# One group of a local-attention kernel with its weights as the stationary operand, and layernorm passes on ScalarE

## The chip, the core and the metric

The kernel runs on one core of a Trainium2 chip. Its engines have names of their own in the profile: PE is TensorE (PEld is its weight load), DVE is VectorE, ACT is ScalarE, POOL is GpSimd, and SP issues most DMAs. The metric is the time of one execution on the device in microseconds, as the median of several runs. Lower is better.

## What is computed

The input x has 2048 rows of 640 numbers, in fp32. Each row is normalised, xn = (x - mean) / sqrt(var + eps). From xn come two branches:

```
qkv  = xn @ wqkv                      # 640 x 1920, 32 heads of 20
each row attends to 8 rows: itself and those 2, 4, ... 14 rows above
s    = attention(q, k, v) @ wo        # 640 x 640
g    = silu( silu(xn @ w1) @ w2 )     # 640 x 1536, 1536 x 640
out  = x + s * g
```

## The kernel before

The 2048 rows are dealt out to four groups of 512 rows, and a group is 4 tiles of 128 rows (T = 4, tile index t). A tile takes every 8th row, so that the 8 rows that a row attends to lie in the same partition of neighbouring tiles or a partition or two above.

For each group the order on TensorE is: the q, k, v product in four quarters (`qkv_phase`), then the output projection of the group before (`wo_phase`), then the FFN (`ffn_phase`). The last group's projection stands at the end by itself (`wo_last`). The attention itself is VectorE's work (products, reductions, sums), spread over the time in which TensorE does the next products.

Precision is kept by splitting. Each operand is a high half of a type that TensorE multiplies fast and a low half that holds what is left. A product is three matmuls: high x high, low x high, high x low. The halves of the activations are TH, TL (normalised input), OH, OL (attention output) and sh, sl (hidden activations); those of the weights stand side by side in a ring of seven buffers `w`. In their first use the weights' halves are made by ScalarE (L463, the high half) and VectorE or POOL (L466, the low half) and stored to DRAM; later uses load the stored halves (L451, on POOL's queue).

In the FFN the first product (`up`, L972 to L974) has the weights stationary and 512 rows of the group moving, 15 matmuls of 512 columns for each of the 12 chunks of 128 hidden units. ScalarE makes silu of the result twice, as the high half sh and in full as sf (L978, L979), and VectorE subtracts to get sl (L980). The second product (`down`) comes for two chunks at a time and has the activations stationary: for each tile t, 640 columns of w2 move in two matmuls, 384 wide (L853) and 256 wide (L856), with the same stationary tile loaded for each. Its result is in rows, over six PSUM banks. The projection has the same form. The result of `down` goes through silu into the tile G (L1027); in `wo_phase` VectorE multiplies the projection into G (L895), POOL adds x (L901), and SP stores the rows (L903).

The next group's x is loaded in the FFN's second pair of chunks. VectorE takes statistics (L500, L502), ScalarE the square root (L506), VectorE applies mean and factor (`ln_apply`, L512). `turn_x` turns the result: VectorE transposes blocks of 32 x 32 (L555), ScalarE moves blocks between partitions (`move`, L540) and makes TH (L524), VectorE makes TL (L525). Attention output is turned the same way in `turn_o` (L567, L540, L524, L525).

The order on each engine is not written out. `Weave` collects the operations with a duration, the tiles read and written and a priority, plays them through in a model, and hands them to the engines in the order in which they started there. TensorE keeps the program's order. Each engine then runs its list strictly in order. A low priority number goes first among operations that could start; layernorm has LN_AT = 55, attention 100 and more, moves 3000.

Of the kernel before, what the change touches and what calls it, by code (L numbers as in the profile page):

```python
# [40 lines left out]
NB = P // B  # L41
SHIFT = 16
RUN = D
X_AT = 1.5, 3.5, 5.5
LOW_AT = 3
ON_DVE = (3, 6, 7, 8)
# [17 lines left out]
def tsl(t):  # L64
    return slice(t * P, (t + 1) * P)
# [175 lines left out]
def local_attention_silu_ffn(ctx: ExitStack, tc: tile.TileContext, x, wqkv, wo, w1, w2, out):  # L241
# [196 lines left out]
    def w_load():  # L438
        i = loaded[0]
        if i >= len(units):  # L440
            return
        loaded[0] += 1
        u, s = units[i], i % RING
        n = width(u)
        r = WR[s]
        both = r[:, :2 * n]
        kh, kl = ("wh", s), ("wl", s)
        due = clock[0]
        if what[i] == "load":
            src = halves[u]  # L450
            add("POOL", 1.0, lambda: nc.gpsimd.dma_start(both, src), [("half", u)], [kh, kl], due + 10,  # L451
                nbytes=2 * n * P * 4)
            return
        k = fresh.index(i)
        if not k:
            raw_load(0)
            rawn[0] = 1
        raw, kr = raws.pop(i)
        early_raw.append((raw, kr))
        hi, lo = r[:, :n], r[:, n:2 * n]  # L460
        if len(raw.shape) > 2:
            hi, lo = (v.rearrange("p (c f) -> p c f", c=DC) for v in (hi, lo))
        act(n, lambda: nc.scalar.activation(hi, raw, AF.Copy), kr, [kh], 1000 + due, name=f"wh{k}")  # L463
        pool_does = k < LO and k not in ON_DVE
        eng, cost, by = ("POOL", po(n), nc.gpsimd) if pool_does else ("DVE", dv(n), nc.vector)
        add(eng, cost, lambda: by.tensor_tensor(  # L466
            out=lo, in0=raw, in1=hi.bitcast(F32), op=OP.subtract), [kh] + kr, [kl],
            due if pool_does else LOW_AT if k < LO else 50, lock=True, name=f"wl{k}")
        if what[i] == "store":
            kept = dram.tile([P, 2 * n], F32, name="half_" + "_".join(map(str, u)))  # L470
            halves[u] = kept
            dma(lambda: nc.sync.dma_start(kept, both.bitcast(F32)), [kh, kl], [("half", u)], 2 * n * P * 4,
                due + STORE)
        while rawn[0] <= (min(k + SLOTS - (k + 1) % 2, early - 1) if k < early - 2 else k + 4):
            raw_load(rawn[0])
            rawn[0] += 1
# [27 lines left out]
    def ln_rstd(a, b, at=1, after=(), name=None):  # L504
        n = range(a, b)
        act(b - a, lambda: nc.scalar.activation(SD[:, 0, a:b], MV[:, a:b, 1], AF.Sqrt, bias=epst, scale=1.0),  # L506
            [("mv", t) for t in n] + list(after), [("sd", t) for t in n], 0, "sqrt", name=name and "q" + name)
        dve(10, lambda: nc.vector.reciprocal(out=SD[:, 1, a:b], in_=SD[:, 0, a:b]),
            [("sd", t) for t in n], [("rs", t) for t in n], at, name=name and "r" + name)

    def ln_apply(t):
        dve(320, lambda: nc.vector.tensor_scalar(  # L512
# [362 lines left out]

    TM = mm(CA) + mm(CB)

    def wo_phase(g, i):
        banks = tm_banks(True)
        a, b = banks  # L880
        for c in range(DC):
# [15 lines left out]
        for t in range(T):  # L897
            s = take("xr", 2)
            xr = XR[s]
            dma(lambda t=t, xr=xr: nc.sync.dma_start(xr, rows(xg, g)[:, t, :]), [], [("xr", s)], P * D * 4, clock[0] + 5)  # L900
            add("POOL", po(D), lambda t=t, xr=xr: nc.gpsimd.tensor_tensor(out=xr, in0=xr, in1=G[:, t, :], op=OP.add),  # L901
                [("g", t, 0), ("g", t, CA)], [("xr", s)], 500, lock=True)
            dma(lambda t=t, xr=xr: nc.sync.dma_start(rows(og, g)[:, t, :], xr), [("xr", s)], [], P * D * 4, clock[0] + 20)  # L903

    def wo_last(g, i):
# [10 lines left out]

        def give(p, kp, t, cs):
            n = cs.stop - cs.start
            dve(n, lambda: nc.vector.tensor_tensor(out=G[:, t, cs], in0=p, in1=G[:, t, cs], op=OP.mult),
                [kp], [("g", t, cs.start)], 0)  # L920
            dve(n, lambda: nc.vector.tensor_tensor(out=xr[t][:, cs], in0=xr[t][:, cs], in1=G[:, t, cs], op=OP.add),
                [("g", t, cs.start)], [kx[t]], 0, lock=True)

        def leave(t, cs):
            dma(lambda: nc.sync.dma_start(rows(og, g)[:, t, cs], xr[t][:, cs]), [kx[t]], [], P * 4 * (cs.stop - cs.start), 0)

        def steps(cs):
            return [(OH, c, k) for c in cs for k in (0, 1)] + [(OL, c, 0) for c in cs]
# [29 lines left out]

    def ffn_phase(g, i, ix, io):
        nxt = g + 1 if g + 1 < NG else None  # L960
        ps = tm_banks()
        a, b = ps

        def up(f):
            wh, wl, kh, kl = w_next("w1", f)
# [3 lines left out]
            def first():  # L969
# [9 lines left out]
            act(TOK, lambda: nc.scalar.activation(sf, h, AF.Silu), [kp], [("sf", s)], 0, "silu")  # L979
            dve(TOK, lambda: nc.vector.tensor_tensor(out=sl, in0=sf, in1=sh.bitcast(F32), op=OP.subtract),  # L980
                [("sf", s), ("sh", s)], [("sl", s)], 0, lock=True)

        def down(fs):
            ws = {f: w_next("w2", f) for f in fs}
# [26 lines left out]
        for f in range(0, FC, 2):  # L1011
# [5 lines left out]
            if nxt is not None and f == X_IN:  # L1017
                for t in range(T):
                    ln_stats(t)
                ln_rstd(0, T, after=[("sf", 1)])  # L1020
                for t in range(T):
                    ln_apply(t)
                turn_x(g, ix)
            down((f, f + 1))
        for p, kp, ts, cs in tm_views(ps, "aaaabb" if nxt is not None else "abaaab"):
            n = (ts.stop - ts.start) * (cs.stop - cs.start)
            act(n, lambda p=p, ts=ts, cs=cs: nc.scalar.activation(G[:, ts, cs], p, AF.Silu), [kp], gkeys(ts, cs), 0.1 if nxt is None else -1, "silu")  # L1027
# [4 lines left out]
    for g in range(NG):  # L1032
        other = 1 - slot
        qkv_phase(g, slot, other)
        if g:
            wo_phase(g - 1, other)
        ffn_phase(g, slot, other, other)
        if g < NG - 1:
            slot = other
# [30 lines left out]
```

## Time and profile before

| | |
|---|---|
| median of 3 runs | 618.46 us (618.18 to 618.94) |
| profiled execution | 618.66 us, span 616.9 us from first to last instruction |
| busy: PE, PEld, DVE, ACT, POOL | 611.0, 551.1, 563.5, 310.4, 110.3 us |
| granted TensorE clock, mean | 0.999 |
| group 0: its FFN, the projection of its rows | 61.06 to 143.39 us, 194.65 to 211.85 us |
| last group: FFN's end and last projection | to 595.9 us, then to 613.3 us |

How to read it: a matmul's duration in the profile runs into the next one's, so a block's length is read from one start to a later start. The chain of waits is the way back from the last instruction through whatever released each step. A row of grouped instructions gives line, engine, operation, tiles, shape and count, then busy time and the mean of one, then the idle time ahead of them and what ended it. A row of the timeline gives start, duration, engine, line.

### The profile page before, as it was taken

The page shows a single profiled execution, that of the slowest core. Times are in us where ns is not written, and L with a number is a line of the kernel's source. Part 1 is how long each engine was busy: PE and PEld are TensorE (multiplying, and loading weights), DVE is VectorE, ACT ScalarE, POOL GpSimd, SP SyncE. Part 2 cuts the span into 40 slices and gives each one's busy share as a digit, 9 for nine tenths or more (in the row PEclk, how much of TensorE's full clock was granted, in tenths as well). Part 3 has the DMA queues.
Part 4 walks back from the last instruction along what each step waited for, and adds up shares of the span by engine and source line. Part 5 has one row for each costly group of instructions (what it writes and reads, how often), then busy time and mean ns, then how long its engine had stood idle before and what let it go on. Part 6 is the DMA issues. An engine that isn't in the chain of part 4 may idle for free.

```text
span 616.9 us, 9054 instructions
## 1 busy us (share of the span) xinstructions
PE 611.0 (99%) x3347; PEld 551.1 (89%) x3347; DVE 563.5 (91%) x584; ACT 310.4 (50%) x656; POOL 110.3 (18%) x167
## 2 busy tenths in 40 slices
PE   8999999999999999999999999999999999999997
PEld 6889999998889999999888999999888999999997
DVE  6578999999989998999999999999979999999964
ACT  5535658937376313851945512582496316152650
POOL 5500000011101133111212233111121213311100
PEclk9999999999999999999999999999999999999999
DMA  8999999867999998764799999955569999866642
GB/s 251 337 281 350 345 371 413 322 222 218 309 295 347 334 358 263 232 198 138 205 240 253 335 333 309 277 179 163 168 198 285 240 320 304 283 213 198 208 149 86
DMA packets 61513, 162.45 MB, mean 263 GB/s; under 512 B 6957, under 2 KB 25229, under 8 KB 61469
## 3 DMA queue, kind: packets, MB, share of 16 engines
q0 software_dynamic: 20016, 82.58, 44.4%
q1 hardware_dynamic: 41453, 79.29, 40.3%
q8 instruction: 26, 0.43, 0.3%
q14 instruction: 18, 0.15, 0.1%
HBM read 109.55 MB, written 34.16 MB: 233 GB/s over the span
## 4 chain that ended last, share of the span: by engine, by line
PE 98%; DMA 1%; DVE 0%; SPq 0%; issue 0%; ACT 0%
PE acc L853 22%; PE acc L856 15%; PE acc L824 10%; PE acc L825 10%; PE acc L826 10%; PE rot L973 9%; PE rot L974 9%; PE rot L972 9%; PE acc L764 2%; DMA xin<-in_A_x_dram 1%; PE rot L856 1%; PE rot L853 0%; PE acc L954 0%; PE rot L729 0%; DVE st L694 0%; PE acc L756 0%
## 5 line engine op out<-in xcount | busy, mean ns | idle before, releaser
L824 PE MATMUL acc<-w,thl 128*128 128x512 f32 (+1 forms) x300 | 112.5, 375 | 0.0
L826 PE MATMUL acc<-w,thl 128*128 128x512 f32 (+1 forms) x300 | 112.4, 375 | 0.0
L825 PE MATMUL acc<-w,thl 128*128 128x512 f32 (+1 forms) x300 | 112.4, 375 | 0.0
L853 PE MATMUL acc<-w,sh 128*128 128x384 f32 x384 | 111.5, 333 | 0.0
L856 PE MATMUL acc<-w,sh 128*128 128x256 f32 x384 | 107.1, 279 | 0.0
L978 ACT ACTIVATE sh<-rot 128x512 fp32r<-128x512 f32 x48 | 28.7, 598 | 146.1 <-PE rot L974 146.0
L974 PE MATMUL rot<-thl,w 128*128 128x512 f32 x240 | 93.6, 390 | 0.0
L973 PE MATMUL rot<-thl,w 128*128 128x512 f32 x240 | 93.6, 390 | 0.0
L972 PE MATMUL rot<-thl,w 128*128 128x512 f32 x240 | 93.5, 389 | 0.0
L662 DVE TENSOR_TENSOR pr<-e,kv 128x2560 f32<-128x2560 f32 x32 | 90.4, 2823 | 0.8
L627 DVE TENSOR_REDUCE l<-pr 128x128 f32<-128x2560 f32 x32 | 90.0, 2813 | 0.6
L624 DVE TENSOR_TENSOR pr<-q,kv 128x2560 f32<-128x2560 f32 x32 | 90.1, 2816 | 0.2
L667 DVE TENSOR_TENSOR pr<-pr 128x1280 f32<-128x1280 f32 x64 | 74.0, 1155 | 1.5
L856 PEld LDWEIGHTS acc<-w,sh 128*128 128x128 f32 x384 | 72.2, 188 | 0.9
L853 PEld LDWEIGHTS acc<-w,sh 128*128 128x128 f32 x384 | 72.1, 188 | 0.9
L451 POOL DMA_DIRECT2D w<-half_w x72 | 38.6, 536 | 190.0 <-PE rot L974 60.8
L451 POOL DMA_DIRECT2D w<-half_q x52 | 27.7, 533 | 242.1 <-PE rot L974 116.8
L824 PEld LDWEIGHTS acc<-w,thl 128*128 128x128 f32 x300 | 56.3, 188 | 8.9 <-ACT gate L1027 0.2
L826 PEld LDWEIGHTS acc<-w,thl 128*128 128x128 f32 x300 | 56.3, 188 | 8.6
L825 PEld LDWEIGHTS acc<-w,thl 128*128 128x128 f32 x300 | 56.3, 188 | 8.6
L853 PE MATMUL acc<-w,thl 128*128 128x384 f32 x225 | 63.1, 333 | 0.0
L540 ACT ACTIVATE xin<-sf 32x256 f32<-32x256 f32 (+1 forms) x144 | 54.6, 379 | 8.2 <-DVE sf L567 6.6
(100 smaller groups left out, 1040.0 us busy)
## 6 DMA issues: line engine op xcount, KB each, us to landing
w<-half_w POOLq DMA_DIRECT2D x72, 640.0 KB, 5.9
w<-half_q POOLq DMA_DIRECT2D x39, 512.0 KB, 4.6
half_w<-w SPq DMA_DIRECT2D x24, 640.0 KB
w<-half_wo POOLq DMA_DIRECT2D x15, 640.0 KB, 5.6
kv<-kv SPq DMA_DIRECT2D x15, 560.0 KB
half_q<-w SPq DMA_DIRECT2D x15, 512.0 KB
kv<-kv SPq DMA_DIRECT2D x15, 420.0 KB
w<-half_q POOLq DMA_DIRECT2D x13, 384.0 KB, 4.9
```

What stands on the lines that cost most here:

```text
L624: dve(2560, lambda t=t: nc.vector.tensor_tensor(out=PR, in0=win(qq[:, t:t + 2, :], W, 0), in1=win(kv[:, 0, t:t + 2, :], W, CQ), op=OP.mult ...
L627: dve(2560, lambda t=t: nc.vector.tensor_reduce(out=l[:, t:t + 2].rearrange("p t w h -> p (t w h)"), in_=PR.rearrange("p t w (h d) -> p (t ...
L662: dve(2560, lambda t=t, v=v: nc.vector.tensor_tensor(out=PR.rearrange("p t w (h d) -> p t (w h) d", d=DH), in0=e[:, t:t + 2].rearrange("p ...
L667: dve(2 * k * CQ, lambda k=k: nc.vector.tensor_tensor(out=PR[:, :, 0:k, :], in0=PR[:, :, 0:k, :], in1=PR[:, :, k:2 * k, :], op=OP.add), [] ...
L824: nc.tensor.matmul(o, hi, wh, start=c == 0, stop=False)
L825: nc.tensor.matmul(o, lo, wh, start=False, stop=False)
L826: nc.tensor.matmul(o, hi, wl, start=False, stop=c == DC - 1)
L853: nc.tensor.matmul(a[t][0][:, :CA], st, w[:, :CA], start=first, stop=last)
L856: nc.tensor.matmul(b[t // 2][0][:, h * CB:(h + 1) * CB], st, w[:, CA:], start=first and h == 0, stop=last, skip_group_check=True)
L972: nc.tensor.matmul(h, wh[:, cs], TH[i][:, c, :], start=c == 0, stop=False)
L973: nc.tensor.matmul(h, wh[:, cs], TL[i][:, c, :], start=False, stop=False)
L974: nc.tensor.matmul(h, wl[:, cs], TH[i][:, c, :], start=False, stop=c == DC - 1)
```

## The change

For group 0 alone (TURNED = 1), the second FFN product and the projection have the weights stationary: for each of the five blocks m of 128 output columns, a block of w2 or wo is loaded, and the group's 512 rows move. Each is 15 matmuls of 512 columns for a chunk of weights, instead of 12 pairs of 384 and 256. The result has output columns on the partitions and rows along the tile, in five PSUM banks. G is used in that form (GT). After the product with the projection, VectorE transposes blocks of 32 x 32 into two scratch rows, POOL adds x to these, and SP loads x and stores the result in four blocks for each tile, since a transpose of 32 x 32 blocks leaves row blocks and column blocks exchanged. To make a block of 32 rows hold adjacent output columns, the columns of w2 and wo are permuted when their halves are made, for all groups. The other groups, whose code is the old one, undo the permutation where x is added and where the last rows are stored.

For all groups that prepare a next one, `ln_apply` on VectorE is replaced by two ScalarE passes for each tile (`ln_apply_act`: add the negated mean, multiply by the factor), with priority LN_PRIO = 3000, and one VectorE instruction that negates the four means.

```diff
+TURNED = 1
+LN_ACT = 1
+LN_PRIO = 3000
...
+        elif u[0] in ("wo", "w2"):
+            hi, lo = (v.rearrange("p (m a b) -> p a m b", a=NB, m=DC) for v in (hi, lo))
+            raw = raw.rearrange("p (a m b) -> p a m b", a=NB, m=DC)
...
+    def ln_apply_act(t):
+        for k in range(2):
+            act(D, lambda k=k: nc.scalar.activation(
+                XIN[:, t, :], XIN[:, t, :], (AF.Identity, AF.Copy)[k], **({"bias": MV[:, t, 0:1]}, {"scale": SD[:, 1, t:t + 1]})[k]),
+                [("rs", t), ("mv", t)], [("xin", t)], LN_PRIO)
...
     def wo_phase(g, i):
+        banks = [bank() for m in range(DC)]
+        for c in range(DC):
+            wh, wl, kh, kl = w_next("wo", c)
+            for m in range(DC):
+                def big(c=c, m=m, wh=wh, wl=wl):
+                    nc.tensor.matmul(banks[m][0], wcols(wh, m), OH[i][:, c, :], start=c == 0, stop=False)
+                    nc.tensor.matmul(banks[m][0], wcols(wl, m), OH[i][:, c, :], start=False, stop=False)
+                pe(2 * mm(TOK), big, t_keys(i, [c], kinds=["th"]) + [kh, kl], [banks[m][1]])
+            for m in range(DC):
+                def small(c=c, m=m, wh=wh):
+                    nc.tensor.matmul(banks[m][0], wcols(wh, m), OL[i][:, c, :], start=False, stop=c == DC - 1)
+                pe(mm(TOK), small, t_keys(i, [c], kinds=["tl"]) + [kh], [banks[m][1]])
+            w_done()
+        for m in range(DC):
+            dve(TOK, lambda m=m: nc.vector.tensor_tensor(out=GT[:, m, :], in0=banks[m][0], in1=GT[:, m, :], op=OP.mult),
+                [banks[m][1]], gmkeys(m), 0)
+        for t in range(T):
...
+            def fetch(t=t, xr=xr):
+                for k in range(NB):
+                    nc.sync.dma_start(xr[:, k * DC * B:(k + 1) * DC * B], blocked(rows(xg, g), g, t, k))
...
+            dve(D, lambda t=t, y=y: nc.vector.transpose(
+                out=y.rearrange("p (i m b) -> p m i b", i=NB, m=DC),
+                in_=GT[:, :, tsl(t)].rearrange("p m (i b) -> p m i b", i=NB)),
+                [k for m in range(DC) for k in gmkeys(m)], [ky], 20)
+            add("POOL", po(D), lambda xr=xr, y=y: nc.gpsimd.tensor_tensor(out=xr, in0=xr, in1=y, op=OP.add),
+                [ky], [kx], 500, lock=True)
+            dma(leave, [kx], [], P * D * 4, clock[0] + 20, dur=1.9)
...
-            dma(lambda: nc.sync.dma_start(rows(og, g)[:, t, cs], xr[t][:, cs]), [kx[t]], [], P * 4 * (cs.stop - cs.start), 0)
+            def go():
+                if cs.stop - cs.start == D:
+                    nc.sync.dma_start(rows(og, g)[:, t, :], xr[t])
+                else:
+                    a, b = cs.start // NB, cs.stop // NB
+                    nc.sync.dma_start(*(v.rearrange("p (a m) -> p a m", a=NB)[:, :, a:b] for v in (rows(og, g)[:, t, :], xr[t])))
+            dma(go, [kx[t]], [], P * 4 * (cs.stop - cs.start), 0)
...
+                if LN_ACT:
+                    dve(4, lambda: nc.vector.tensor_scalar(out=MV[:, :, 0], in0=MV[:, :, 0], scalar1=-1.0, scalar2=None, op0=OP.mult),
+                        [("rs", t) for t in range(T)], [("mv", t) for t in range(T)], LN_AT)
                 for t in range(T):
-                    ln_apply(t)
+                    (ln_apply_act if LN_ACT else ln_apply)(t)
                 turn_x(g, ix)
-            down((f, f + 1))
+            (down if straight else down_turned)((f, f + 1))
```

`down_turned` is to `down` what the new `wo_phase` is to the old one: for the two chunks first the matmuls of sh with both halves of w2 (L1070, L1071), then those of sl (L1081). The old `wo_phase` lives on as `wo_straight`.

Three places show what moves. The first is TensorE's list at the first down product of group 0 (acc are the PSUM banks, sh_82 the hidden activations, w_75 a chunk of w2). Before:

```order
L974 MATMUL rot_112<-thl_67,w_74 128x512
L853 MATMUL acc_109<-w_75,sh_82 128x384
L856 MATMUL acc_107<-w_75,sh_82 128x256
L853 MATMUL acc_109<-w_75,sh_82 128x384
L856 MATMUL acc_107<-w_75,sh_82 128x256
L853 MATMUL acc_110<-w_75,sh_82 128x384
```

With the change:

```order
L1054 MATMUL rot_112<-thl_67,w_74 128x512
L1070 MATMUL acc_109<-sh_82,w_75 128x512
L1071 MATMUL acc_109<-sh_82,w_75 128x512
L1070 MATMUL acc_110<-sh_82,w_75 128x512
L1071 MATMUL acc_110<-sh_82,w_75 128x512
L1070 MATMUL acc_105<-sh_82,w_75 128x512
```

Pairs of 384 and 256 became matmuls of 512, and what moves and what stands still changed places.

The second place is ScalarE's list from the middle of group 0's FFN on (chunks 8 and 9; sh_82 and sh_83 are the high halves of silu, xin<-kv are the moves of `turn_x`, thl_71 is the next group's TH). Before:

```order
L540 ACTIVATE xin<-kv_89 32x640 x3
L463 ACTIVATE w_80<-gate 128x640
L540 ACTIVATE xin<-kv_89 32x640 x3
L524 ACTIVATE thl_71<-xin 128x512
L978 ACTIVATE sh_82<-rot_111 128x512
L979 ACTIVATE sf<-rot_111 128x512
L524 ACTIVATE thl_71<-xin 128x512 x4
L978 ACTIVATE sh_83<-rot_112 128x512
L979 ACTIVATE sf<-rot_112 128x512
L463 ACTIVATE w_74<-gate 128x640
```

With the change (from chunk 9 to chunk 11):

```order
L1058 ACTIVATE sh_83<-rot_112 128x512
L1059 ACTIVATE sf<-rot_112 128x512
L469 ACTIVATE w_75<-gate 128x4x5x32
L552 ACTIVATE xin<-kv_89 32x640 x8
L469 ACTIVATE w_77<-raw 128x512
L552 ACTIVATE xin<-kv_89 32x640 x3
L1058 ACTIVATE sh_82<-rot_111 128x512
L1059 ACTIVATE sf<-rot_111 128x512
L469 ACTIVATE w_79<-raw 128x512
L552 ACTIVATE xin<-kv_89 32x640
L536 ACTIVATE thl_71<-xin 128x512 x2
L1058 ACTIVATE sh_83<-rot_112 128x512
```

The moves and the splits of the next group's input have gone from chunks 8 and 9 to chunks 10 and 11, the last ones; three more splits stand behind the rows shown.

The third place is VectorE's list at the end of group 0's projection (acc are its banks, gate is G, sl_84 and sl_85 the low halves of the next group's first two chunks). Before:

```order
L627 TENSOR_REDUCE l_97<-pr 128x128
L895 TENSOR_TENSOR gate<-acc_109,gate 128x384
L895 TENSOR_TENSOR gate<-acc_110,gate 128x384
L895 TENSOR_TENSOR gate<-acc_105,gate 128x384
L895 TENSOR_TENSOR gate<-acc_106,gate 128x384
L895 TENSOR_TENSOR gate<-acc_107,gate 128x2x256
L895 TENSOR_TENSOR gate<-acc_108,gate 128x2x256
L652 TENSOR_REDUCE z_87<-e_98 128x32
L654 RECIPROCAL z_87<-z_87 128x32
L980 TENSOR_TENSOR sl_84<-sf,sh_82 128x512
L980 TENSOR_TENSOR sl_85<-sf,sh_83 128x512
```

With the change:

```order
L917 TENSOR_TENSOR gate<-acc_109,gate 128x512
L917 TENSOR_TENSOR gate<-acc_110,gate 128x512
L931 STREAM_TRANSPOSE raw<-gate 128x5x4x32 x2
L664 TENSOR_REDUCE z_87<-e_98 128x32
L666 RECIPROCAL z_87<-z_87 128x32
L931 STREAM_TRANSPOSE raw<-gate 128x5x4x32
L1060 TENSOR_TENSOR sl_84<-sf,sh_82 128x512
L1060 TENSOR_TENSOR sl_85<-sf,sh_83 128x512
L931 STREAM_TRANSPOSE raw<-gate 128x5x4x32
L667 TENSOR_TENSOR e_98<-e_98,z_87 128x256
L639 TENSOR_REDUCE l_97<-pr 128x128
```

Three transposes now stand ahead of the low halves, and the long reduction of the attention stands behind all of it.

60 lines of the change are left out of this document (55 added, 5 removed).

## The prediction

> **What bounds the kernel now.** I read the page first: its busy line, its slices, and the chain that ended last.
>
> ```profile
> PE 611.0 (99%) x3347; PEld 551.1 (89%) x3347; DVE 563.5 (91%) x584; ACT 310.4 (50%) x656; POOL 110.3 (18%) x167
> ...
> PEclk9999999999999999999999999999999999999999
> ...
> PE 98%; DMA 1%; DVE 0%; SPq 0%; issue 0%; ACT 0%
> ```
>
> TensorE runs at its full granted clock in every slice, and 98% of the chain is TensorE. VectorE is 91% busy too, so the next view is who TensorE waited for (the weight loads' queue included).
>
> ```profile
> PE rot L680 <- POOL ident masks.py:199: 1.4, 1, 1.4
> PE rot L729 <- DVE xin L700: 0.7, 2, 0.4
> PE acc L756 <- DMA pr<-in_A_wqkv_dram: 0.2, 1, 0.2
> ...
> PEld acc L824 <- ACT gate L1027: 0.2, 1, 0.2
> ```
>
> All waits but the last lie in the first 11 us; the last is one stop of 0.2 us. So no work of VectorE, ScalarE or a queue sets the end now. Three things do: the number and price of matmuls, any wait that the change makes, and the tail behind the last matmul.
>
> **The matmuls.** These rows of TensorE's timeline are one pair of hidden chunks in group 0: the up product (512 columns), the down product (384 and 256 in turn), the next up product.
>
> ```profile
> 74.79 0.39 PE L972 MATMUL rot<-thl,w 128*128 128x512 f32 x1
> ...
> 76.64 0.39 PE L974 MATMUL rot<-thl,w 128*128 128x512 f32 x1
> ...
> 81.62 0.34 PE L853 MATMUL acc<-w,sh 128*128 128x384 f32 x1
> ...
> 88.51 0.39 PE L972 MATMUL rot<-thl,w 128*128 128x512 f32 x1
> ...
> 95.34 0.34 PE L853 MATMUL acc<-w,sh 128*128 128x384 f32 x1
> ```
>
> The duration in the second column overlaps with the next matmul, so only differences of starts count. From 81.62 to 88.51 there are 24 pairs of 384 and 256: 6.89 us, 287 ns for 640 columns. From 88.51 to 95.34 there are 30 matmuls of 512: 6.83 us, 227.7 ns each. Inside such a block the price is not even: the first eight (74.79 to 76.64) take 231 ns each, the next 22 (76.64 to 81.62) 226.4 ns. 640 columns in full-width matmuls therefore cost 1.25 x 226.4 = 283.0 to 1.25 x 227.7 = 284.6 ns, against 287. The change gains 2.5 to 4 ns per 640 columns, since 255 matmuls do the columns of 408: the columns themselves cost the same.
>
> ```profile
> 61.06:143.39 82.33, 82.33 (x469) 1.00 0.92 330
> 194.65:211.85 17.20, 17.20 (x121) 1.00 1.11 343
> ```
>
> These are group 0's whole FFN and its output projection (window, its length, TensorE's busy time). The FFN becomes 360 matmuls of 512: 81.50 us at 226.4 ns, 81.97 at 227.7, so 0.36 to 0.83 us less. The projection becomes 75 of them: 16.98 to 17.08 us, 0.12 to 0.22 less. The eight slow matmuls behind each run of narrow pairs cost 8 x 4.9 ns = 0.04 us; the blocks behind the two changed products, the next group's first and the FFN's first, may lose them: 0 to 0.08. The sum is 0.48 to 1.13 us. I take 0.8, the middle: the moving data change sides, but a 512-column matmul costs the same with either operand moving in the rows I have.
>
> [...]
>
> **Layernorm on ScalarE.** Twelve VectorE instructions go; 24 ScalarE passes and 3 tiny negations come. Price from rows of the grouped view:
>
> ```profile
> L512 DVE TENSOR_SCALAR xin<-xin,mv,sd 128x640 f32<-128x640 f32 x12 | 6.5, 610 | 0.1
> L463 ACT ACTIVATE w<-xr 128x640 fp32r<-128x640 f32 x8 | 5.9, 737 | 5.2 <-issue 3.0 <-PE acc L826 2.2
> L555 DVE STREAM_TRANSPOSE gate<-xin 128x640 f32<-128x640 f32 x8 | 6.0, 811 | 1.6 <-POOL xr L901 1.6
> L895 DVE TENSOR_TENSOR gate<-acc,gate 128x512 f32<-128x512 f32 x6 | 3.8, 681 | 0.0
> ...
> L540 ACT ACTIVATE xin<-kv 32x640 f32<-32x640 f32 x16 | 11.8, 737 | 0.2
> ...
> L627 DVE TENSOR_REDUCE l<-pr 128x128 f32<-128x2560 f32 x32 | 90.0, 2813 | 0.6
> ```
>
> VectorE loses 6.5 us and gains four transposes (4 x 0.81) in the projection; its five products (5 x 0.68 = 3.4 us) replace six that took 3.1. Net about 3 us less, worth nothing directly, as TensorE never waits for it. ScalarE gains 24 x 0.74 = 18 us; it is 50% busy. What hides this is its idle time while it waits for the up product. What it could cost is a late silu: ScalarE works in order, and behind a layernorm pass stand the silu that TensorE's down product reads, and the splits of the next group's input.
>
> ```profile
> 121.27 2.19 ACT L524 ACTIVATE thl<-xin 128x512 fp32r<-128x512 f32 x4
> ...
> 123.84 0.60 ACT L979 ACTIVATE sf<-rot 128x512 f32<-128x512 f32 x1
> ...
> 133.35 0.60 ACT L978 ACTIVATE sh<-rot 128x512 fp32r<-128x512 f32 x1 [3.98 <-PE rot L974]
> ...
> 136.70 0.60 ACT L978 ACTIVATE sh<-rot 128x512 fp32r<-128x512 f32 x1 [1.75 <-PE rot L974]
> ```
>
> The splits end at 123.5 now and are needed from 143.4 on: 20 us of room. In the new order the last three stand behind the last silu pair of group 0, so they end near 136.7 + 1.2 + 3 x 0.55 = 139.6. The later chunks are read 2.7 us apart (12 matmuls of 227 ns), so 3 us or more are left. A silu of an even chunk has the following up product (3.4 us) as room, one of an odd chunk the first ten matmuls of the down product (2.3 us). The longest queue in group 0's new order lies ahead of the silu of chunk 10: behind chunk 9's silu (done at 124.4) stand two weight conversions and eleven moves of 0.74 us, 9.6 us, so it starts near 134.0 instead of 133.35, 0.65 late out of 3.4. So I charge 0; the bounds are 0 and, for places that I have not added up, 2 us.
>
> **Projection of group 0.** Its products wait for the last matmuls as before, then two transposes stand ahead of the low halves of the silu, and the third transpose waits for POOL's addition, since there are two scratch rows.
>
> ```profile
> 213.49 3.14 DVE L895 TENSOR_TENSOR gate<-acc,gate 128x384 f32<-128x384 f32 x6
> ...
> 216.29 3.08 POOL L901 TENSOR_TENSOR xr<-xr,gate 128x640 f32<-128x640 f32 x2
> ...
> 217.49 3.21 DVE L980 TENSOR_TENSOR sl<-sf,sh 128x512 fp32r<-128x512 f32 x2
> ...
> 218.88 0.60 ACT L978 ACTIVATE sh<-rot 128x512 fp32r<-128x512 f32 x1 [2.31 <-PE rot L974]
> ```
>
> The products move ahead of a 2.8 us reduction (L627 above), so they start near 211 and end near 214.5. Two transposes end at 216.1, POOL's first addition (1.5 us) at 217.7, the third transpose at 218.5, and the second low half waits for its silu (218.88 + 1.1) and ends near 220.7. The down product reads it 20 matmuls behind 218.8, near 223.3. Two microseconds are left: charge 0. The x rows and results of this group go in four DMAs for each one, 24 more issues on SP at some 0.33 us (a row below), in a stretch where nothing is read from them by TensorE: 0.
>
> **The tail.** Columns are permuted now, so the last tile leaves in pieces of 96 and 64 columns.
>
> ```profile
> 613.81 0.42 DVE L921 TENSOR_TENSOR xin<-xin,gate 128x256 f32<-128x256 f32 x1
> 614.26 0.33 SPq L925 DMA_DIRECT2D out_dram<-xin  x1
> ...
> 12.60:13.20 0.60, 0.60 (x5) 0.48 (x4) 0.60 (x3) 0.00 (x0) 0.60 (x1) 1.00 0.96 298
> 613.40:614.50 1.10, 0.00 (x0) 0.00 (x0) 0.80 (x2) 0.00 (x0) 0.00 (x0) 1.00 0.49 179
> 614.90:615.70 0.80, 0.00 (x0) 0.00 (x0) 0.00 (x0) 0.00 (x0) 0.00 (x0) 0.83 0.48 164
> ```
>
> ```profile
> DMA packets 284, 0.18 MB, mean 298 GB/s; under 512 B 19, under 2 KB 284, under 8 KB 284
> ```
>
> The last two numbers of a window are the busy share of the 16 DMA engines and GB/s. The last transfer (128 packets of 1 KB) takes 0.48 of 0.8 us = 0.38 us. It becomes 512 packets of 256 B. The nearest stretch of short packets, 12.6 to 13.2 (the second fence), moved 284 in 0.6 us, all under 2 KB: 512 at that pace take 1.08 us, 0.7 more. If only bytes counted it would be 0 more. I take 0.35. The transfer ahead of it (512 packets of 384 B) starts near 613.5 and at the same pace ends near 614.6, before the last one starts.
>
> **Sum.** -0.8 + 0.35 = -0.45 us on the profiled execution: 618.66 becomes 618.2, its span 616.9 becomes 616.45 (1.76 us lie around the span). The median of the runs, 618.46, is 0.2 below that execution; so 618.0.
>
> **Rivals.** (1) Faster by more than the forecast: all bounds fall well, no tail cost, and the 0.2 us stop for ScalarE's gate goes as well. 618.46 - 1.13 - 0.22 = 617.1. For it: the page shows nothing else on the chain. Against: it needs every term at its end, and nothing that the change frees on VectorE can turn into time.
>
> [...]
>
> (3) Slower through ScalarE: a layernorm pass whose input from VectorE comes late holds a silu, and TensorE stops. VectorE's 2.8 us instructions set the size: one such delay beyond the 2.3 us of room is 0.5 us, and three groups with two such places each give up to 3: about 620.5 with the other terms. For it: ScalarE and VectorE now hand the same tile back and forth four times for each group. Against: the room worked out above.
>
> (4) The change does not lower the matmul price: weight loads set the pace of the narrow pairs, and the wide ones with the activations moving are no cheaper for 640 columns. 618.46 + 0.35 = 618.8.
>
> ```profile
> L853 PEld LDWEIGHTS acc<-w,sh 128*128 128x128 f32 x384 | 72.1, 188 | 0.9
> ```
>
> For it: weight loads are busy 89% of the span at 188 ns each. Against: two of them fit into a pair's 287 ns, so they overlap, and the up product (activations moving) already shows 226 to 228 ns.
>
> **How the numbers follow.** The smallest change that this kernel's measurement can tell from none is about 0.2%, 1.24 us: faster is below 617.2, slower above 619.7. Chances: forecast 0.5, (1) 0.15, (2) 0.1, (3) 0.1, (4) 0.15. (1) is faster: 0.15. (2) and (3) are slower: 0.2. The forecast and (4), 0.65, can't be told from no change. The range runs from (1), less 0.2 for the spread of the runs, to between (2) and (3): 616.9 to 620.1.
>
> **What would show it.** In the profile after: L1070, L1071 and L1081 start 226 to 228 ns apart, and group 0's FFN takes 81.5 to 82.0 us. TensorE's waits show nothing on L978's successor or the splits past 20 us. The window behind the last VectorE instruction is 0 to 0.7 us longer. Wrong would be: starts at 231 ns or more, a wait of TensorE for ScalarE over 0.5 us, or last packets of 256 B that take 60 ns and more.

## The result, and the profile after

The changed kernel takes 629.76 us (median of 4 runs, 627.99 to 630.78), beside 618.44 (618.18 to 618.94) for the kernel before on the same chip: 1.0178 times as long, 95% interval 1.0165 to 1.019. The forecast was 618.0 with a range up to 620.1. The change makes the kernel slower, by 11.3 us, and not in the way of any rival.

The profiled execution took 629.31 us; its span is 10.7 us longer than before. Its page, against the lines shown of the kernel before:

```profile
span 627.5 us, 8787 instructions
...
PE 615.3 (98%) x3194; PEld 542.7 (86%) x3194; DVE 558.6 (89%) x578; ACT 328.4 (52%) x679; POOL 110.5 (18%) x167
...
PEclk9999999999999997999999999999999999999999
...
PE 67%; DMA 18%; DVE 8%; SPq 3%; issue 2%; ACT 2%; DVEq 0%; ACTq 0%
```

TensorE was 98% of the chain and is 67% now; transfers are 18%. One slice, the sixteenth, has a lower clock. The view by windows of the three FFN phases that were 82.33, 82.32 and 82.43 us long (window, its length, busy time of TensorE; the granted clock stands third from the end):

```profile
61.31:144.12 82.81, 82.67 (x362) 67.50 (x361) 80.41 (x84) 59.11 (x93) 2.28 (x4) 1.00 0.94 336
212.57:301.47 88.90, 85.41 (x469) 77.45 (x468) 76.80 (x82) 41.59 (x66) 19.11 (x28) 0.96 0.74 228
369.93:455.56 85.63, 82.94 (x470) 75.22 (x469) 76.00 (x74) 41.87 (x64) 19.80 (x28) 1.00 0.70 222
```

Group 0's FFN, the one that was changed, is only 0.48 us longer. Group 1's is 6.58 us longer and group 2's 3.20, and in both of them TensorE runs the same products as before. With 0.25 us at the start and 0.29 behind the last matmul this makes 10.8; 0.1 us came back between groups 2 and 3, where the stop for ScalarE's gate is gone. So the loss is in the work behind the change. The page of waits says who is late:

```profile
POOL xr L935 <- DMA xr<-in_A_x_dram: 18.0, 3, 8.9
...
DVE st L506 <- DMA xin<-in_A_x_dram: 9.2, 3, 7.8
...
DVE raw L931 <- POOL xr L935: 7.4, 2, 6.3
PEld acc L865 <- DVE sl L1060: 7.3, 4, 2.9
```

(What waited, for whom, us in total, times, longest.) TensorE waits for the low halves of the silu, VectorE for POOL and for the input, POOL for the added x rows. In group 1 the timelines of VectorE and of TensorE give the order:

```profile
218.60 0.85 DVE L931 STREAM_TRANSPOSE raw<-gate 128x640 f32<-128x640 f32 x1 [1.14 <-POOL xr L935]
...
227.66 0.84 DVE L931 STREAM_TRANSPOSE raw<-gate 128x640 f32<-128x640 f32 x1 [6.28 <-POOL xr L935]
...
239.78 0.68 DVE L1060 TENSOR_TENSOR sl<-sf,sh 128x512 fp32r<-128x512 f32 x1
```

```profile
237.58 0.28 PE L868 MATMUL acc<-w,sh 128*128 128x256 f32 x1
240.53 0.69 PE L865 MATMUL acc<-w,sl 128*128 128x384 f32 x1 [2.66 <-DVE sl L1060]
...
242.61 0.41 PE L868 MATMUL acc<-w,sl 128*128 128x256 f32 x1
243.85 0.69 PE L865 MATMUL acc<-w,sl 128*128 128x384 f32 x1 [0.82 <-DVE sl L1060]
```

The fourth transpose waits 6.28 us, and everything that stands behind it on VectorE waits too; the low half that TensorE reads next is written at 239.78 (230.38 before). The fourth transpose needs a scratch row that POOL's second addition reads, and that addition waits for the second x row. The chain names the transfer, and SP's timeline (SPq is its queue, and the duration is the time that issuing takes) what stands behind it. SP before, then SP after, then three pieces of the chain after:

```profile
193.30 0.48 SPq L900 DMA_DIRECT2D xr<-in_A_x_dram  x1
...
195.75 3.21 SPq L592 DMA_DIRECT2D kv<-kv  x4
...
206.52 0.91 SPq L492 DMA_DIRECT2D xin<-in_A_x_dram  x2
```

```profile
192.78 3.69 SPq L925 DMA_DIRECT2D xr<-in_A_x_dram  x4
...
200.32 12.55 SPq L925 DMA_DIRECT2D xr<-in_A_x_dram  x4
212.97 5.68 SPq L604 DMA_DIRECT2D kv<-kv  x4
...
219.94 2.01 SPq L498 DMA_DIRECT2D xin<-in_A_x_dram  x2
```

```profile
200.93 1.61 SPq L925
202.59 18.96 DMA xr<-in_A_x_dram
221.57 13.47 DMA xin<-in_A_x_dram
```

The second x row took SP 12.55 us to issue, for four DMAs of 80 KB that I had put at some 0.33 us each. The four halo copies (kv<-kv, which bring the attention's neighbouring rows into a partition) and the two loads of the next input stand behind it and start 17 and 13 us later than before. Of the row's four pieces the third landed 19 us after its issue began, as the chain shows; by the trace's record of landings the last came at 225.86, and POOL's addition began at 226.07. Why is it so slow? One stretch, 254 to 257 us, holds almost nothing but these fetches. Its row by windows, and the page of transfers for it:

```profile
254.00:257.00 3.00, 3.00 (x23) 3.00 (x22) 2.27 (x3) 2.96 (x5) 0.92 (x1) 1.00 0.28 87
```

```profile
DMA packets 421, 0.26 MB, mean 87 GB/s; under 512 B 12, under 2 KB 421, under 8 KB 421
...
q1 hardware_dynamic: 421, 0.26, 28.5%
```

The fetches alone keep 0.28 of the 16 engines busy, at 87 GB/s. In the projection's window of the kernel before the share reads 1.11, and a quarter of 1.11 is 0.28. The DMA's pattern is 4 blocks of 32 rows of 640 B. That such a fetch is the work of four of the 16 engines was the author's estimate from these two shares. Another reading was open at this point: 512 packets of 640 B instead of 128 of 2,560 B, each waiting its turn behind the weights' packets.

### The profile page after: what moved, and what is told of

Read it like the earlier page. It is cut to its first block, busy times and chain, and to the rows that moved or that the text cites. A ratio compares the mean times of both kernels' runs of the same rounds, so it can differ in the third digit from the quotient of the medians.

```text
span 627.5 us, 8787 instructions
## 1 busy us (share of the span) xinstructions
PE 615.3 (98%) x3194; PEld 542.7 (86%) x3194; DVE 558.6 (89%) x578; ACT 328.4 (52%) x679; POOL 110.5 (18%) x167
## 4 chain that ended last, share of the span: by engine, by line
PE 67%; DMA 18%; DVE 8%; SPq 3%; issue 2%; ACT 2%; DVEq 0%; ACTq 0%
PE acc L865 12%; PE acc L868 8%; PE acc L838 7%; PE rot L1052 7%; PE acc L836 7%; PE acc L837 7%; PE rot L1053 7%; PE rot L1054 7%; DMA xin<-in_A_x_dram 6%; DMA kv<-kv 4%; DMA xr<-in_A_x_dram 3%; DVE pr L636 2%; PE acc L1081 2%; PE acc L776 2%; PE acc L1071 1%
## 5 line engine op out<-in xcount | busy, mean ns | idle before, releaser
L865 PE MATMUL acc<-w,sh 128*128 128x384 f32 x288 | 83.6, 333 | 0.0
L868 PE MATMUL acc<-w,sh 128*128 128x256 f32 x288 | 80.3, 279 | 0.0
L868 PEld LDWEIGHTS acc<-w,sh 128*128 128x128 f32 x288 | 54.1, 188 | 0.7
L865 PEld LDWEIGHTS acc<-w,sh 128*128 128x128 f32 x288 | 54.1, 188 | 0.7
L1054 PEld LDWEIGHTS rot<-thl,w 128*128 128x128 f32 x240 | 45.2, 188 | 9.7
```

The lines of the kernel that those rows point to most:

```text
L865: nc.tensor.matmul(a[t][0][:, :CA], st, w[:, :CA], start=first, stop=last)
L868: nc.tensor.matmul(b[t // 2][0][:, h * CB:(h + 1) * CB], st, w[:, CA:], start=first and h == 0, stop=last, skip_group_check=True)
L1054: nc.tensor.matmul(h, wl[:, cs], TH[i][:, c, :], start=False, stop=c == DC - 1)
```

## The experiments

The theories: **A**, four engines for each fetch, which hold SP's queue and make the x rows, the halo rows and the next input late. **B**, the number of packets. **C**, the layernorm on ScalarE. **D**, the transposes' place on VectorE.

### The same DMAs cut the other way

```diff
-        return view[k * B:(k + 1) * B, t, :].rearrange("u (a m) -> a u m", a=NB)
+        return view[:, t, k * DC * B:(k + 1) * DC * B].rearrange("(i u) m -> u i m", i=NB)
...
-                    nc.sync.dma_start(xr[:, k * DC * B:(k + 1) * DC * B], blocked(rows(xg, g), g, t, k))
+                    nc.sync.dma_start(xr[k * B:(k + 1) * B, :].rearrange("u (i m) -> u i m", i=NB), blocked(rows(xg, g), g, t, k))
```

and the same for the stores. A slice of 32 partitions takes the place of a slice of columns.

> The changed kernel, with group 0's x rows and results cut into four DMAs for each tile in the other direction: each moves 32 partitions of 4 x 640 B instead of 4 blocks of 32 rows; bytes, number of DMAs (32 + 32... that is 16 fetches and 16 stores), packets (512 of 640 B for a tile) and the order of every engine stay as they are. Theory A (a DMA whose slowest dimension is 4 uses only 4 of the 16 engines, as the windows with 0.28 to 0.29 busy and 87 to 88 GB/s suggest; that holds SP's queue, and the x rows, the halo rows and the next input all come 10 us late): the stop of 6 to 7 us in group 1's FFN goes, 622 to 623.5, or 618.5 to 620 if the stops of group 2's FFN (1.67 + 1.34 us) hang on it too; SP's four fetches of a tile issue in about 2 us, not 3.7 and 12.6. Theory B (it is the number of packets: each short packet waits its turn behind the weights' packets of 5 KB): no change, 629 to 630.5. Theory C (the layernorm on ScalarE makes VectorE late): no change, 629 to 630.5. Theory D (VectorE's transposes, which stand in its order ahead of the low halves, are to blame, wherever x comes from): at most 1 us less, 629.

620.81 us, 1.0039 times the kernel before (1.0025 to 1.0052). SP and the wait that is left:

```profile
196.34 4.77 SPq L925 DMA_DIRECT2D xr<-in_A_x_dram  x4
201.20 6.83 SPq L604 DMA_DIRECT2D kv<-kv  x4
...
211.09 0.96 SPq L498 DMA_DIRECT2D xin<-in_A_x_dram  x2
```

```profile
PEld acc L865 <- DVE sl L1060: 1.4, 1, 1.4
```

The same DMAs, bytes and 640 B packets, with the same order on every engine: 9 us less. Group 1's FFN is 82.30 us. B, C and D fall as causes of the large stop. Of group 2's two stops one is left (1.4 us), so the time lies between the two sums of theory A. The pages of the two kernels, first the changed one, differ in the short packets:

```profile
DMA packets 65352, 162.43 MB, mean 259 GB/s; under 512 B 7981, under 2 KB 30093, under 8 KB 65309
```

```profile
DMA packets 65737, 162.44 MB, mean 263 GB/s; under 512 B 8366, under 2 KB 30478, under 8 KB 65694
```

385 more are under 512 B, twelve for each of the 32 DMAs (384 of them have 4 bytes). The trace's record of landings fits: a piece of a row in the 4-block form lands in four parts (the last piece of the second row at 220.94, 221.31, 221.33 and 225.86 us), one in the 32-partition form in sixteen. So four shares against sixteen is shown by the landings, and not only estimated from the shares of two windows.

### The two forms in the kernel before

```diff
+    def carry_x(g, t, xr, get):
+        if g:
+            pairs = [(xr, rows(xg if get else og, g)[:, t, :])]
+        else:
+            v = rows(xg if get else og, g)
+            pairs = [(xr[:, k * 160:(k + 1) * 160], v[k * 32:(k + 1) * 32, t, :].rearrange("u (a m) -> a u m", a=4)) for k in range(4)]
```

Its twin has the 32-partition pairs in the last line. Both have the same order on every engine. In both, group 0's x is added and its result stored in permuted places, so group 0's output is not the one asked for; the amount of work is.

> The kernel before, only group 0's x rows and results go in the changed kernel's form: four DMAs for each tile, 4 blocks of 32 rows by 640 B each (the added x of group 0 is thereby taken from permuted places, and stored back in the same permutation, so the gate's product lands in other columns of group 0's output; all else is as before). No transposes, no turned products, layernorms on VectorE. Theory A: the late halo rows and the late input alone stop TensorE in group 1's FFN: 622 to 628. Theory B (packets): the same, 622 to 628. Theory C and D: no change, 618 to 619.5.

> The kernel before with group 0's x rows and results in the 32-partition form (for x and result alike permuted, so that group 0's gate meets other columns of x; all else is as before): as many DMAs and packets as in the 4-block run of the kernel before, the same order on every engine. Theory A (4 engines against 16): 618.5 to 621. Theory B (packets of 640 B waiting their turn): 628 to 631, as with 4 blocks.

With 4 blocks 630.89 us (1.0193, 1.0173 to 1.0213), with 32 partitions 618.46 (0.9998, 0.9989 to 1.0007). The second x row on SP, first with 4 blocks, then with 32 partitions:

```profile
200.69 11.28 SPq L885 DMA_DIRECT2D xr<-in_A_x_dram  x4
```

```profile
196.64 2.83 SPq L885 DMA_DIRECT2D xr<-in_A_x_dram  x4
```

This alone, in a kernel with no turned product, no transposes ahead of the low halves and the layernorms on VectorE, costs 12.4 us between the twins (12.0 against the kernel before of its own round). Of the 12.9 us between their profiled spans 10.8 lie in group 1's FFN; 2.1 lie ahead of the first of these fetches and can't be theirs. Four times the packets cost nothing that can be measured. The size was above the 622 to 628 that I expected: here the late x row holds VectorE as well, through the transposition of the next input, whose scratch POOL's addition reads (9.8 us in one wait), and TensorE stops three times between 238 and 262 us, for 1.6, 2.1 and 3.7 us, and runs at half clock for 6.8 us.

### Fetches and stores apart

```diff
-                    nc.sync.dma_start(xr[:, k * DC * B:(k + 1) * DC * B], blocked(rows(xg, g), g, t, k))
+                    nc.sync.dma_start(xr[k * B:(k + 1) * B, :].rearrange("u (i m) -> u i m", i=NB), across(rows(xg, g), t, k))
```

Only the fetch; across() is the 32-partition cut of the first experiment.

> The changed kernel with only the fetches of group 0's x rows in the 32-partition form; the stores of its results stay in the 4-block form. If the fetch is what makes group 1's FFN late (it stands ahead of the halo rows and the input on SP, and POOL and VectorE wait for it), the first stop goes as in the first experiment: 620.5 to 622.5. If the slow stores matter as much (the next two fetches stand behind them on SP, and each x buffer comes free only when its store is through), stops of 1 to 3 us stay between 240 and 270 us: 622.5 to 626.

620.65 us (1.0037, 1.0026 to 1.0048), as with both in that form; the order on every engine is the changed kernel's. No stop of TensorE is left in group 1; the 2.3 us by which group 2's FFN is too long are the matter of the input loads below. The slow stores take SP 15.0 us (eight issues from 217.73 on), and nothing that TensorE waits for comes too late behind them. So the price of the 4-block form is the fetches': 629.76 against 620.65.

### The second fetch behind the halo rows and the input

```diff
-            dma(fetch, [], [kx], P * D * 4, clock[0] + 5, dur=1.9)
+            dma(fetch, [("halo", NQ - 1, tag, h, 0) for tag in (1, 2) for h in (0, 112)] if t else [], [kx], P * D * 4, clock[0] + 40, dur=1.9)
```

> The changed kernel with its 4-block DMAs, only the fetch of group 0's second x tile stands behind the four halo loads and the two input loads of group 1 on SP, not ahead of them (and group 2's two input loads then stand together behind its halo loads). Theory A1 (the slow fetches hold SP's queue, and the halo rows and the input that stand behind them come late): those are issued 10 us earlier, and group 1's stop of 6 to 7 us shrinks to under 3: 622 to 626. Theory A2 (what is late is the x row itself: POOL's addition waits for it, VectorE's third transpose for POOL, and everything behind it on VectorE): no gain, 628 to 631.

623.26 us (1.0083, 1.0067 to 1.0099), in the range of A1, but the stops in group 1 did not fall below 3 us: they are 3.1 and 1.2. SP and VectorE:

```profile
200.42 5.04 SPq L604 DMA_DIRECT2D kv<-kv  x4
...
207.16 3.20 SPq L498 DMA_DIRECT2D xin<-in_A_x_dram  x2
213.29 12.98 SPq L925 DMA_DIRECT2D xr<-in_A_x_dram  x4
```

```profile
227.78 0.89 DVE L506 BATCH_NORM_STATS2 st<-xin 128x6 f32<-128x320 f32 x2 [4.36 <-DMA xin<-in_A_x_dram]
...
239.76 0.85 DVE L931 STREAM_TRANSPOSE raw<-gate 128x640 f32<-128x640 f32 x1 [4.17 <-POOL xr L935]
```

Both links are real. With the queue free the halo rows and the input are issued 13 us earlier, and 6.5 of the 11.3 us go; the late x row still holds the fourth transpose for 4.17 us. The edit does more than its text says: Weave then put VectorE's list in another order too, with the fourth transpose behind the input's statistics, so the 6.5 us are both moves together. The input, though issued at 207.16, is awaited until 227.78. The record of landings tells why: of the first load's sixteen parts eleven are in by 217.85, and the last four come between 222.49 and 227.75. Four late parts are as many as the 4-block fetches have, which were issued from 213.29 to 226.27; that they share engines is the likely reason, but the record does not name the engine of a part.

### The layernorm's place

The changed kernel with LN_ACT = 0, the changed kernel with TURNED = 0, and the kernel before with only this:

```diff
                 for t in range(T):
-                    ln_apply(t)
+                    ln_apply_act(t)
```

with the negation of the means ahead of it, as in the change.

> The changed kernel with the layernorms left on VectorE (12 operations of 0.61 us, no passes on ScalarE); group 0's products are turned and its x rows go in 4-block DMAs as in the change. In its written order of SP the two loads of group 2's input stand together behind eight halo loads, where the changed kernel has one ahead of four and one behind. Theory A and B: group 1's stop stays, so 626 to 630.5 (group 2's stops may go: then 626 to 627). Theory C: 618 to 620. Theory D: 629 to 630.

> The changed kernel with no group turned: all groups' products as before, x rows in one DMA for a tile, layernorms on ScalarE, and the columns of wo and w2 permuted as in the change (so the last stores are in pieces of 384 and 256 B). Theory A and B: none of group 1's stop, 618 to 620, the layernorm's and the tail's own cost being what stands above 618.5. Theory C: 624 to 630. Theory D: 618 to 620.

> The kernel before with the layernorms' application on ScalarE and nothing else of the change: no permuted weights or stores, no turned products. The forecast charged 0 for this part (bounds 0 to 2 us): 618.2 to 619. The run with this part and the permutation took 618.7; its window behind the last matmul is 0.3 us longer than the kernel before's (4.13 against 3.83), so without the permutation 618.2 to 618.6, and a window of 3.8.

631.97 us (1.0208, 1.0173 to 1.0243), 618.72 (1.0, 0.9991 to 1.001) and 618.22 (0.9995, 0.9987 to 1.0004). C falls: the move costs nothing. With the layernorms on VectorE the turned kernel (group 0's products in the new form) is no faster than with them on ScalarE; 631.97 is above the range given for A, and the intervals of the two overlap. The permutation's price shows in the window from the start of the last matmul to the end of the span: 4.13 us in the second run, which has it, 3.83 in the third, which has not.

### Group 2's stops

The loads in question bring the input that is prepared in group 2's FFN, that is, group 3's x. In the written order of the changed kernel one of the two stands ahead of four halo copies and one behind them; before, both stood ahead (from 346.02, the copies from 347.05). SP's rows after, and VectorE's:

```profile
353.96 0.40 SPq L498 DMA_DIRECT2D xin<-in_A_x_dram  x1
354.47 3.16 SPq L604 DMA_DIRECT2D kv<-kv  x4
357.68 0.53 SPq L498 DMA_DIRECT2D xin<-in_A_x_dram  x1
```

```profile
380.89 0.89 DVE L506 BATCH_NORM_STATS2 st<-xin 128x6 f32<-128x320 f32 x2 [7.85 <-DMA xin<-in_A_x_dram]
```

```diff
-                load_x(nxt, 0, 2)
-                load_x(nxt, 2, 2)
+                load_x(nxt, 0, 2, clock[0] - 60)
+                load_x(nxt, 2, 2, clock[0] - 60)
```

on top of the first experiment. On SP this moves that load and, at the start of the program, one of group 1's input (from 21.1 to 16.3 us). Weave then also ordered VectorE's and ScalarE's lists in group 2's FFN anew.

> The 32-partition form of the first experiment, and the second load of group 2's input put ahead of the four halo loads in SP's order, where it stands in the kernel before; nothing else moves. Theory A' (what is left over the kernel before, 1.38 us in one stop of group 2's FFN, is that load: issued at 350.6 instead of 347.3, with VectorE waiting 5.9 us for it): the stop goes, 619.2 to 619.6. Rival: the load lands late however early it is issued, because the 16 engines are busy throughout that stretch: 620.5 to 621. If the turned products themselves were 0.8 us cheaper than before, it would end at 618.3 or less; by their spacing in the first experiment (229.7 ns) they are not, and nothing below 618.8 is expected.

618.93 us (1.001, 1.0001 to 1.0019); group 2's FFN and SP's loads:

```profile
363.50:445.82 82.32, 82.32 (x470) 75.16 (x469) 77.83 (x76) 42.03 (x64) 19.17 (x28) 1.00 0.74 228
```

```profile
347.54 0.92 SPq L498 DMA_DIRECT2D xin<-in_A_x_dram  x2
```

The stop is gone, and the time is a little under the range given. With a load of 640 KB issued 3 to 4 us later, behind four copies, group 2's FFN had lost 1.4 us in the first experiment and, with a further stop, 3.2 in the changed kernel. How much of it is the load and how much the order planned around it, this run does not separate. The kernel is now 0.5 us above the one before: 0.3 lie behind the last matmul, and group 0's FFN has a stop of its own for a low half, 0.1 to 1.1 us in six of the seven profiles with turned products and layernorms on ScalarE, none in the one that has only the fetches cut anew. The kernel before with 4 blocks has it too (1.1 us), so it is not the turned product's alone; its cause is open.

### The price of a turned matmul

In the first experiment, one pair of hidden chunks of group 0, TensorE's timeline:

```profile
95.53 0.40 PE L1070 MATMUL acc<-sh,w 128*128 128x512 f32 x1
...
102.42 0.40 PE L1052 MATMUL rot<-thl,w 128*128 128x512 f32 x1
...
104.73 0.39 PE L1053 MATMUL rot<-thl,w 128*128 128x512 f32 x1
```

30 turned matmuls in 6.89 us: 229.7 ns each, where 226.4 to 227.7 was forecast. The ten behind them take 231 ns, so the slow ones that followed the narrow pairs are still there. Two edits asked why. The first does all high weights of a chunk ahead of all low ones, so that the accumulator changes with each matmul:

```diff
                         nc.tensor.matmul(ps[m][0], wcols(wh, m), sh, start=f == 0, stop=False)
-                        nc.tensor.matmul(ps[m][0], wcols(wl, m), sh, start=False, stop=False)
...
+                for m in range(DC):
+                    def low(m=m, f=f, sh=sh, wl=wl):
+                        nc.tensor.matmul(ps[m][0], wcols(wl, m), sh, start=False, stop=False)
+                    pe(mm(TOK), low, [ksh, kh, kl], [ps[m][1]])
```

The second takes the projection in threes, with the operands in the sequence of the FFN's first product:

```diff
                     nc.tensor.matmul(banks[m][0], wcols(wh, m), OH[i][:, c, :], start=c == 0, stop=False)
-                    nc.tensor.matmul(banks[m][0], wcols(wl, m), OH[i][:, c, :], start=False, stop=False)
...
+                    nc.tensor.matmul(banks[m][0], wcols(wh, m), OL[i][:, c, :], start=False, stop=False)
+                    nc.tensor.matmul(banks[m][0], wcols(wl, m), OH[i][:, c, :], start=False, stop=c == DC - 1)
```

> The kernel of the run above, only the turned second product of group 0's FFN does the high parts for all five blocks of columns first and then the low parts, so its 240 large matmuls change their accumulator after every one and not after every second. Theory P (the 229 to 232 ns of a turned matmul, against 227 in the first product, is the price of changing the accumulator): the starts of L1070's successor and of the low parts go from 229.7 to about 232 ns, 0.5 us more in group 0's FFN. Rival Q (it comes with the moving data being the same for ten matmuls in a row, or with anything else that this edit leaves): 229 to 230 ns as in the run above, no change.

> The kernel of the fifth run (32 partitions, input loads first), only the turned output projection of group 0 now takes, for each block of columns, high weight by high half, high weight by low half, low weight by high half, three in a row into one accumulator: the same stationary and moving sequence as the FFN's first product, which takes 227 ns. If the 229 ns of the turned products come from the moving data staying the same for ten matmuls, the 75 matmuls fall to 227 ns and the projection from 17.2 to 17.0 us. If not (the accumulators that change, the many blocks), it stays at 229 and 17.2.

618.78 us (1.0008, 1.0 to 1.0017), and 620.18 (1.0026, 1.0015 to 1.0036), the latter with a stop of 0.8 us in its projection, which its own order makes. The mean distance of starts stays: 229.5 ns in the FFN of the first and 229.2 in the projection of the second, where the run that both start from has 229.5 and 229.0 (stops left out). The first edit was to cost 0.5 us by its theory; it concerns 120 matmuls and not 240, so 0.28 was the price to look for, and the distance, which was to go to 232, shows none of it. Neither the change of accumulators nor the repeated moving data is the reason; it stays open.

## Why the prediction was wrong, step by step

**What bounds the kernel** was read rightly, and so was its use: any wait that the change makes is paid in full. The wait was looked for in the wrong places.

**"The x rows and results of this group go in four DMAs for each one, 24 more issues on SP at some 0.33 us (a row below), in a stretch where nothing is read from them by TensorE: 0."** This is the step that failed. Its price was wrong: 0.9 and 3.1 us for each issue of the first two rows, since the pattern of the DMA was not looked at and a row of another shape gave the price. Its cover was wrong too: TensorE reads nothing from the rows, but POOL does, VectorE waits for POOL in its order, and on SP the halo rows and the next input stand behind. Cut to 32 partitions, the same four DMAs take the time from 629.76 to 620.81: 9 us hang on that word "0". None of the four rivals was this mechanism.

**The order around it.** That the written order would split the two input loads in group 2's part was not looked for; it stood on SP, two groups behind the edit. With the fetches mended, the run that puts them together, and with it the plan's order around them, is 1.9 us faster (620.81 to 618.93), or 1.5 when each is set against the kernel before of its own round.

**VectorE's schedule in the projection** was sound as far as it went: the third transpose was to start when POOL's first addition is done, at about 217.7, and to end at 218.5; it began at 218.60 after 1.14 us of waiting, and the low halves came in time. The fourth transpose, which needs the second x row, was not in the reckoning.

**The matmuls, -0.8 us (-0.48 to -1.13).** Mis-sized: nothing. The run with no stop in group 0's FFN has

```profile
60.87:143.28 82.41, 82.41 (x362) 67.52 (x361) 80.31 (x86) 52.51 (x83) 2.29 (x4) 1.00 0.93 331
```

82.41 us against 82.33, and the projection with the matmul ahead of it is 17.35 against 17.38. Rival (4) had this term right: the wide matmuls with the activations moving are no cheaper for 640 columns. They take 229.0 to 229.7 ns, where the rows from which they were priced have 226.4 to 227.7. Its reason, that weight loads set the pace of the narrow pairs, no run tests; but what was said against it does not come out, since two loads of 188 ns are 376 ns, more than the 287 of a pair. That "a 512-column matmul costs the same with either operand moving" was an assumption that no row shown bore out for these operands: 229.7 x 1.25 is 287 ns for 640 columns, as much as the old pair.

**The layernorm on ScalarE, 0:** right (618.22 against 618.49, and 618.72 against 618.84 with the permutation). Rival (3) did not come: the stops are waits for VectorE's low halves, not for a silu. (Its time does not follow from its terms: 3 us more than the forecast's 618.0 are 621.0, not 620.5.)

**The tail, +0.35 (0 to 0.7):** right, 0.3. In the changed kernel the last transfer shows as

```profile
625.50:626.30 0.80, 0.00 (x0) 0.00 (x0) 0.00 (x0) 0.00 (x0) 0.00 (x0) 0.75 0.75 164
```

0.75 of 0.8 us busy, 0.60 against 0.38 before, for the same 128 KB in four times the packets. The 0.1 for rival (2) and in part the upper end of the range (620.1) took in a much dearer last transfer: no run shows such a cost, and what the runs show in its place is this 0.22 us more of busy time and the 0.3 us by which the window behind the last matmul grew.

## What to carry to other kernels

When a transfer is cut up or its pattern turned, price the pattern, not the count, and look up in how many parts a piece lands: here pieces of 4 blocks landed in four parts and cost 9 us and more, and pieces with 32 partitions outermost, with the same bytes and packets, landed in sixteen (629.76 against 620.81 us). A DMA that "nobody waits for" was not free here: VectorE waited 6.28 us for POOL's addition, which reads the row, and the halo copies behind the transfer on SP's queue were issued 17 us later; follow both. After an edit to a planned order, compare the queues over the whole program, since a load that slipped behind four copies two groups later, with the order planned around it, was worth 1.5 to 1.9 us here. And compare the order on every engine between an experiment and its base: here the two edits that name one transfer each moved much else.

## What the runs showed of the hardware that was not expected

After some stops TensorE's clock fell to half. In the changed kernel:

```profile
236.78:240.19 3.41, 1.08 (x8) 0.82 (x6) 3.38 (x4) 0.30 (x1) 0.00 (x0) 1.00 0.46 167
240.19:247.02 6.83, 5.67 (x19) 5.08 (x20) 6.80 (x7) 2.98 (x4) 0.89 (x2) 0.50 0.52 148
```

A stop of 2.8 us was followed by 6.83 us at a granted clock of 0.50, with a second stop of 1.1 us in it; about 2.6 of group 1's 6.6 us are this slower pace. Stops of 1.3 to 1.7 us in group 2 had no such sequel, nor had one of 3.1 us (238.14 to 241.23) in the run with the late fetch:

```profile
236.10:239.51 3.41, 2.21 (x16) 1.95 (x14) 0.00 (x0) 0.00 (x0) 1.31 (x1) 1.00 0.29 86
239.51:242.92 3.41, 1.69 (x10) 1.64 (x11) 3.16 (x3) 0.00 (x0) 1.27 (x3) 1.00 0.68 200
```

So the length of a stop alone does not decide. The windows shown are cut in steps of 3.41 us: in the traces' records of the granted clock every stretch between two changes is a whole multiple of 3.41 us (half clock for 3.41, 6.83 and 13.65, full clock for 235.52 or 610.99, say). Counted on in steps of 3.41 from a trace's first change, what TensorE worked in a step told whether half clock followed, in all thirteen profiles up to the last matmul: at full clock, steps with 1.50 us of work or less (1.50, 1.08, 0.66, 0.35) were followed by half clock, and steps with 1.69 us or more were not. The 3.1 us stop fell across two steps and left 2.21 and 1.69 us of work in them.

Packets of 640 B instead of 2,560 B, four times as many, cost nothing measurable in the 32-partition form (0.9998, 0.9989 to 1.0007), in a stretch where the share of the 16 engines reads 1.04 in the kernel before (192 to 205 us).
